# Loading wq by two transfers, over 16 and over 112 rows, in a one-token attention and gated-MLP kernel

## The chip, the cores and the metric

The kernel runs on one core of one Trainium2 chip. Time is the device time in microseconds of one execution, of which three runs of the kernel before are given. A core has five engines with instruction streams of their own (PE for matmuls, DVE, ACT and POOL for element-wise work, SP, which here only issues transfers) and 16 DMA engines which carry the transfers that SP and ACT issue.

## The reference

One token for each of two batch rows. x (2 x 448) is normalized; q = xn @ wq has 16 heads of 256. Attention goes over the last W = 2048 positions of a cache with 8 key and value heads, each used by two query heads; the result, 2 x 4096, is multiplied by wo. Beside it a small MLP of the same normalized x, with silu, gates that product:

```
xn = layernorm(x)
q = (xn @ wq).reshape(B, 1, 16, 256)
scores = q . k_cache[:, :, 8192 - 2048:] * 256 ** -0.5     # heads repeated twice
o = softmax(scores) . v_cache[:, :, 8192 - 2048:]
s = o.reshape(B, 1, 4096) @ wo
g = silu(relu(xn @ w1) @ w2)
out = x + s * g
```

All inputs are bf16. wq is 448 x 4096, w1 448 x 1792, w2 1792 x 448, wo 4096 x 448; the used part of each cache is 2 x 8 x 2048 x 256.

## The kernel before, in words

The work consists mostly in bringing 44 MB into the core's memory: 16.8 MB of keys, 16.8 MB of values, 3.67 MB each of wq and wo, 3.2 MB of w1 and w2. Keys and values come in NQ = 4 rounds of 4 (batch, head) pairs, each round a K tile and a V tile of 128 partitions x 16,384 bf16 (4 MB). There are two buffers for K (kbuf) and two for V (vbuf). The weights borrow them: wq lies in the second V buffer, w1 and w2 in the first, and wo in the first K buffer, after its last K tile has been used.

The order of the instructions on each engine is written out by hand: a small recorder, `_Prog`, appends operations to one list per engine with the operations that they depend on, and `run` turns the dependences into semaphore waits. Each transfer has a semaphore of its own. An operation that waits holds up everything behind it on its engine, SP's issues included. All operations recorded through one helper carry that helper's line in the profile: transfers L36, most matmuls L249.

SP issues all large transfers, in this order: wq (L194), w1 and w2 (L195, L196), K0 and K1, then V0, which waits for the last matmul that reads w1 and w2, then K2, V1, K3, V2, V3 and wo in four parts (L510 to L514), each after the buffer that it overwrites has been read. ACT issues the two loads of x at the beginning and the store of the result.

wq is seen as 896 half rows of 2048, seven of them (SLOTS) on each partition, so that a partition gets one contiguous run of 7 x 2048 bf16 = 28,672 bytes of the matrix:

```
wq_src = A_wq.rearrange("r (hf c) -> (r hf) c", hf=2).rearrange("(p s) c -> p (s c)", s=SLOTS)
```

The steps that wq touches: DVE normalizes x and PE spreads it over the partitions (xr, L255). `do_q` (L261) then waits for wq, xr and a zeroed PSUM bank and runs 28 matmuls that make q, two rescalings on DVE into kt, 16 small matmuls, a copy to qall, and POOL's copies into the block-diagonal stationary tiles qbd. After it on PE come the MLP's matmuls (`do_H`, `do_hT`, `do_F`). Then for each round k: DVE transposes the K tile in eight steps (L343, `do_T`), PE multiplies each by qbd into a score bank (`do_S`), a chain over DVE, PE and ACT takes maximum and exponential, and PE multiplies with the V tile (`do_PV`). The last matmuls (L528) multiply by wo as its four parts land; two DVE operations and a store follow.

Of the kernel before, what the change touches and what calls it, by code (L numbers as in the profile page):

```python
# [11 lines left out]
PE, DVE, ACTE, SP, POOL = "pe", "dve", "act", "sp", "pool"  # L12
# [62 lines left out]
def bass_recurrent_scan__sliding_block_cached__dense_activation_relu__decode_kernel(  # L75
# [24 lines left out]
    SLOTS = 7  # L100
    HC = HD // 2
# [7 lines left out]
    with es:  # L109
        pr = _Prog(nc, es)  # L110
# [7 lines left out]
        def view(t, off, dims, n=128, p0=0, pstep=1):  # L118
            width = t.shape[1]
            return bass.AP(t, p0 * width + off, [[width * pstep, n]] + dims)  # L120
# [42 lines left out]
        wq_sb, w12, wo_sb = vbuf[1], vbuf[0], kbuf[0]  # L163
# [18 lines left out]
        wq_src = A_wq.rearrange("r (hf c) -> (r hf) c", hf=2).rearrange("(p s) c -> p (s c)", s=SLOTS)  # L182
# [8 lines left out]
            d_v[k] = pr.dma(SP, vbuf[k % 2][:, :], kv_src(k, A_v_cache),  # L191
                            [(st["F"], st["q_mm"])[k] if k < 2 else st["PV", k - 2]])

        d_wq = pr.dma(SP, wq_sb[:, 0:SLOTS * HC], wq_src)  # L194
        d_w1 = pr.dma(SP, w12[:, 0:W2], w1_src)  # L195
        d_w2 = pr.dma(SP, w12[:, W2:W2 + 14 * D].rearrange("p (hf f) -> p hf f", hf=2), w2_src)  # L196

# [12 lines left out]
        a_z = [pr.op(ACTE, lambda e, t=t: e.memzero(t[:, :])) for t in (obk[0], obk[1], fbk)]  # L210
# [37 lines left out]
        def mm(out_ap, lhsT, rhs, start, stop=False, **kw):  # L248
            return lambda e: e.matmul(out_ap, lhsT=lhsT, rhs=rhs, start=start, stop=stop,  # L249
                                      skip_group_check=True, **kw)  # L250

        for s in range(SLOTS):
            m_xr = pr.op(PE, mm(mbk[:, 2 * s:2 * s + 2], xg[0:B, 128 * s + 128:128 * s + 256], ident[0:B, 0:B], s == 0),
                         [v_xn, p_id])
        v_xr = pr.op(DVE, lambda e: e.tensor_tensor(  # L255
            out=view(xr, 0, [[4, SLOTS], [2, 2], [1, 2]]), in0=view(mbk, 0, [[2, SLOTS], [0, 2], [1, 2]]),
            in1=view(par8, 0, [[1, SLOTS], [1, 2], [0, 2]]), op=ALU.mult), [m_xr, v_par8])
# [1 line left out]
        st = {"mbk": v_xr}  # L259

        def do_q():  # L261
            deps = [d_wq, v_xr, a_z[0]]
            for s in range(SLOTS):
                for i in range(4):
                    lo = s * HC + i * 512
                    o = pr.op(PE, mm(obk[0][32 * i:32 * i + 4, :], xr[:, 4 * s:4 * s + 4], wq_sb[:, lo:lo + 512],
                                     s == 0, s == SLOTS - 1, tile_position=(0, 32 * i)), deps)
                    deps = []
            st["q_mm"] = o
            for par in range(2):  # L270
                v = pr.op(DVE, lambda e, par=par: e.tensor_scalar(  # L271
                    out=view(kt, 128 * par, [[256, 8], [32, 4], [1, 32]]),
                    in0=view(obk[0], par, [[64, 8], [0, 4], [2, 32]]),
                    scalar1=SCALE, scalar2=None, op0=ALU.mult), [o])
            st["osb", -2] = v
            deps = [v, p_id]
            for h in range(2):
                for cp in range(8):
                    n = 8 * h + cp
                    o = pr.op(PE, mm(nbk[:, 16 * n:16 * n + 16], kt[:, 128 * n:128 * n + 128],  # L280
                                     view(ident, 0, [[2, 2], [32, 4], [1, 2]]), h == 0 and cp == 0,
                                     h == 1 and cp == 7), deps)
                    deps = []
            st["qT"] = o
            st["qall"] = st["nbk"] = pr.op(DVE, lambda e: e.tensor_copy(
                view(qall, 0, [[1, 2], [2, 8], [16, 16]]), view(nbk, 0, [[128, 2], [16, 8], [1, 16]])), [o])
# [169 lines left out]
        load_k(0)  # L456
        load_k(1)
        do_q()
        do_H(0)
        do_H(1)  # L460
# [55 lines left out]
        deps = [st["at", NQ - 1], v_fold]  # L516
        for b in range(2):
            m_at = pr.op(PE, mm(mbk[:, 256 + 32 * b:288 + 32 * b], at_exp[:, 128 * b:128 * b + 128],
                                fold[:, :], b == 0, b == 1), deps + [st["mbk"]])
            deps = []  # L520
        v_at2 = pr.op(DVE, lambda e: e.tensor_copy(at2[:, :], mbk[:, 256:320]), [m_at])  # L521
        deps = [v_at2, st["g"]]
        landed = dict(d_wo)
        for j in range(32):
            deps = deps + [landed.get(j)]
            for i in range(4):
                lo = j * D + i * NCOL
# [3 lines left out]
                deps = []  # L531
# [37 lines left out]
```

## Time and profile before

| | |
|---|---|
| median of three runs | 110.84 us (110.48 to 110.93) |
| the profiled execution | 110.73 us, span 109.3 us |
| moved over SP's queue (q1) | 44.11 MB, 94.6% of 16 engines' span |
| mean rate over the span | 404 GB/s |
| busy PE, DVE, ACT, POOL | 58%, 53%, 11%, 8% of the span |
| granted TensorE clock | 0.875 |

The span goes from the first to the last instruction; the profiled execution's own time is 1.4 us longer than its span. The views used are: the page with its 40 slices, its table of DMA queues and the chain that ended last; the stages (busy time of each engine, DMA share and rate in stretches that one chooses, where a packet is counted in the stretch in which it starts); the instructions in order of time; and the waits. A transfer is cut into packets, which here are one partition's contiguous run each.

### The profile page before, as it was taken

What the parts mean: (1) busy time and instruction counts of PE and PEld (TensorE: products, weight loads), DVE (VectorE), ACT (ScalarE), POOL (GpSimd) and SP (SyncE); (2) the same over time, 40 slices, a digit from 0 to 9 for tenths busy, and PEclk for the clock granted to TensorE, in tenths of its full rate; (3) what the DMA queues carried; (4) which work ended last, traced back from release to release, by engine and by line L of the source; (5) the groups of instructions that cost most, each with busy time, mean ns of one, the idle gap of its engine ahead of it and who ended that gap; (6) DMA issues with size and microseconds to landing.
All of it is one profiled execution on the core that took longest, in us unless ns stands there. A gap on an engine that the chain in (4) does not pass through costs nothing.

```text
span 109.3 us, 1328 instructions
## 1 busy us (share of the span) xinstructions
PE 63.9 (58%) x554; PEld 26.0 (24%) x554; DVE 57.6 (53%) x95; ACT 12.4 (11%) x24; POOL 9.0 (8%) x45
## 2 busy tenths in 40 slices
PE   0010655764089897849481999683089949009491
PEld 0000113133033222323130334241034214003190
DVE  2165047320399999987435999242399943100202
ACT  2970000000000000200050000032000004100200
POOL 6500000720000004000500000000000000000000
PEclk9999999999556999999996559999959999955559
DMA  6898999999999999999999999999999999999940
GB/s 169 346 483 355 431 404 510 408 432 504 390 396 444 492 396 396 456 480 396 399 480 438 396 408 492 432 396 408 504 420 396 420 498 408 396 405 414 407 171 1
DMA packets 2321, 44.19 MB, mean 404 GB/s; under 512 B 266, under 2 KB 396, under 8 KB 908
## 3 DMA queue, kind: packets, MB, share of 16 engines
q1 hardware_dynamic: 2288, 44.11, 94.6%
q8 instruction: 4, 0.07, 0.2%
q10 hardware_dynamic: 28, 0.01, 0.0%
q14 instruction: 1, 0.01, 0.0%
HBM read 44.11 MB, written 0.00 MB: 403 GB/s over the span
## 4 chain that ended last, share of the span: by engine, by line
DMA 70%; DVE 12%; PE 12%; SPq 3%; issue 1%
DMA kbuf<-in_A_k_cache_dram 42%; DMA kbuf<-in_A_wo_dram 28%; DVE kt L343 10%; PE sbk L249 9%; SPq L36 3%; PE obk L249 2%; DVE tmp L331 1%; DVE rm L361 1%; PE mbk L249 0%; PE nbk L249 0%; PE fbk L249 0%; DVE mx L371 0%; DVE tmp L532 0%; PE mbk L366 0%; DVE out_sb L534 0%
## 5 line engine op out<-in xcount | busy, mean ns | idle before, releaser
L249 PE MATMUL sbk<-kt,qbd 128*128 128x512 bf16 x128 | 36.2, 432 | 15.0 <-DVE kt L343 14.5
L343 DVE STREAM_TRANSPOSE kt<-kbuf 128x1024 f32<-128x1024 f32 x32 | 36.9, 1210 | 8.9 <-DMA kbuf<-in_A_k_cache_dram 8.7
L249 PEld LDWEIGHTS sbk<-kt,qbd 128*128 128x128 bf16 x128 | 12.3, 107 | 37.2 <-DVE kt L343 22.5
L249 PE MATMUL obk<-vbuf,pt 128*16 128x512 bf16 x128 | 9.3, 442 | 4.6 <-DMA vbuf<-in_A_v_cache_dram 4.6
L292 POOL COPY qbd<-qall 32x32 bf16<-32x32 bf16 x32 | 5.7, 204 | 44.1 <-PE sbk L249 28.3
L383 ACT ACTIVATE bias<-mbk 128x1 f32<-128x1 f32 x4 | 0.7, 171 | 58.6 <-PE mbk L249 58.6
L433 DVE TENSOR_TENSOR at_exp<-nbk,qmask 128x16 bf16<-128x16 f32 x16 | 1.7, 166 | 10.5 <-PE nbk L249 10.5
L249 PE MATMUL obk<-vbuf,xr 128*4 128x512 bf16 x28 | 3.2, 626 | 3.8 <-DMA vbuf<-in_A_wq_dram 3.8
L392 DVE STREAM_TRANSPOSE pt<-e_sb 128x512 bf16<-128x512 bf16 x4 | 2.8, 711 | 4.7 <-ACT e_sb L387 4.7
L271 DVE TENSOR_SCALAR kt<-obk 128x1024 bf16<-128x1024 f32 x2 | 2.4, 1218 | 5.6 <-PE obk L249 5.6
L249 PEld LDWEIGHTS obk<-vbuf,pt 128*16 128x16 bf16 x128 | 3.1, 98 | 8.5 <-DMA vbuf<-in_A_v_cache_dram 4.7
L249 PE MATMUL mbk<-ident,xg 2*128 2x2 bf16 x7 | 0.3, 164 | 7.9 <-DVE xg L219 7.9
L361 DVE TENSOR_REDUCE rm<-sbk 128x1 f32<-128x512 f32 x4 | 2.7, 682 | 4.0 <-PE sbk L249 4.0
L249 PE MATMUL fbk<-vbuf,xr 128*4 128x448 bf16 x14 | 4.3, 461 | 0.7 <-DVE h_n L304 0.7
L416 ACT ACTIVATE o_sb<-obk,rs 128x512 bf16<-128x512 f32 x4 | 2.7, 687 | 11.1 <-PE obk L249 11.1
L249 PE MATMUL fbk<-kbuf,at 128*17 128x112 bf16 x128 | 3.1, 282 | 0.4 <-DVE at L521 0.3
L249 PEld LDWEIGHTS fbk<-kbuf,at 128*17 128x17 bf16 x128 | 2.7, 128 | 0.7 <-DVE at L521 0.4
L304 DVE TENSOR_SCALAR h_n<-fbk 4x448 bf16<-4x448 f32 x2 | 1.2, 612 | 3.0 <-PE fbk L249 3.0
L387 ACT ACTIVATE e_sb<-sbk,bias 128x512 bf16<-128x512 f32 x4 | 2.7, 687 | 0.1
L249 PE MATMUL mbk<-one_f,mrow 1*128 1x1 f32 x8 | 1.5, 256 | 1.9 <-DVE mrow L374 1.9
L366 PE MATMUL mbk<-ident_f,rm 128*1 128x128 f32 x4 | 1.1, 270 | 2.4 <-DVE rm L361 2.4
L249 PE MATMUL nbk<-fold,o_sb 128*128 128x8 bf16 x16 | 1.0, 170 | 2.2 <-ACT o_sb L416 2.2
(63 smaller groups left out, 34.4 us busy)
## 6 DMA issues: line engine op xcount, KB each, us to landing
kbuf<-in_A_k_cache_dram SPq DMA_DIRECT2D x4, 4096.0 KB, 27.0
vbuf<-in_A_v_cache_dram SPq DMA_DIRECT2D x4, 4096.0 KB, 26.4
vbuf<-in_A_wq_dram SPq DMA_DIRECT2D x1, 3584.0 KB, 11.2
vbuf<-in_B_w_dram SPq DMA_DIRECT2D x2, 1568.0 KB, 16.2
kbuf<-in_A_wo_dram SPq DMA_DIRECT2D x1, 1904.0 KB, 28.2
kbuf<-in_A_wo_dram SPq DMA_DIRECT2D x1, 1008.0 KB, 30.0
kbuf<-in_A_wo_dram SPq DMA_DIRECT2D x1, 448.0 KB, 30.6
kbuf<-in_A_wo_dram SPq DMA_DIRECT2D x1, 224.0 KB, 30.7
```

What stands on the lines that cost most here:

```text
L36: o = _Op(eng, lambda e: e.dma_start(dst, src), [d for d in deps if d is not None], True)
L249: return lambda e: e.matmul(out_ap, lhsT=lhsT, rhs=rhs, start=start, stop=stop, skip_group_check=True, **kw)
L271: v = pr.op(DVE, lambda e, par=par: e.tensor_scalar(out=view(kt, 128 * par, [[256, 8], [32, 4], [1, 32]]), in0=view(obk[0], par, [[64, 8], ...
L292: st["qbd", k] = pr.op(POOL, lambda e, a=a, b=b: e.tensor_copy(view(qbd[k % 2], 24 + 32 * a + 4 * b, [[2, 2], [128, 8], [1, 2]], n=32, p0= ...
L304: st["h_n"] = pr.op(DVE, lambda e: e.tensor_scalar(out=h_n[0:4, u * (FC // 2):(u + 1) * (FC // 2)], in0=fbk[0:4, 0:FC // 2], scalar1=0.0, ...
L343: st["T", k, e] = pr.op(DVE, lambda e: e.transpose(view(dst, lo, [[128, NT // 2], [1, 32]]), view(src, lo, [[128, NT // 2], [1, 32]])), deps)
L361: st["rm", k] = pr.op(DVE, lambda e: e.tensor_reduce(out=rm[k % 2][:, :], in_=sbk[k % 2][:, :], axis=AX.X, op=ALU.max), [st["S", k, 7], st ...
L366: st["rmT", k] = pr.op(PE, lambda e: e.matmul(mbk[0:1, 0:128], lhsT=rm[k % 2][:, :], rhs=ident_f[:, :], start=True, stop=True, is_transpos ...
L387: st["exp", k] = pr.op(ACTE, lambda e: e.activation(e_sb[k % 2][:, :], sbk[k % 2][:, :], ACT.Exp, bias=bias[k % 2][:, 0:1], accum_out=ssum ...
L392: st["pt", k] = pr.op(DVE, lambda e: e.transpose(pt[k % 2][:, :], e_sb[k % 2][:, :]), [st["exp", k], st.get(("PV", k - 2))])
L416: st["osb", k] = pr.op(ACTE, lambda e: e.activation(o_sb[k % 2][:, :], obk[k % 2][:, :], ACT.Copy, scale=rs[:, k:k + 1]), [st["PV", k], st ...
L433: st["at", k] = st["nbk"] = pr.op(DVE, lambda e, b=b, h=h: e.tensor_tensor(out=view(at_exp, 128 * b + 64 * h + 16 * k, [[4, 2], [8, 2], [1 ...
```

## The change

The transfer of wq is issued as two: the first over partitions (rows of wq_src) 0 to 15, the second over 16 to 127. `do_q`, the only reader, waits for both. The number of DMA engines is 16, so the first has one row for each and the second seven.

```
-        d_wq = pr.dma(SP, wq_sb[:, 0:SLOTS * HC], wq_src)
+        d_wq = [pr.dma(SP, wq_sb[lo:hi, 0:SLOTS * HC], wq_src[lo:hi, :]) for lo, hi in ((0, 16), (16, 128))]
         d_w1 = pr.dma(SP, w12[:, 0:W2], w1_src)
...
         def do_q():
-            deps = [d_wq, v_xr, a_z[0]]
+            deps = [*d_wq, v_xr, a_z[0]]
```

SP's list grows by one issue, ahead of w1. The other engines' instructions and their order are the same, but for the wait on one more semaphore ahead of the first matmul of `do_q`.

## The prediction

> **What bounds the kernel now.** I read the page first: span, the lines of DMA by slices, the queues, the chain that ended last.
>
> ```profile
> span 109.3 us, 1328 instructions
> ...
> DMA  6898999999999999999999999999999999999940
> ...
> q1 hardware_dynamic: 2288, 44.11, 94.6%
> ...
> DMA 70%; DVE 12%; PE 12%; SPq 3%; issue 1%
> ```
>
> The 16 DMA engines work in nine tenths or more of nearly every slice, and SP's queue (q1) alone fills 94.6% of sixteen engines' span with 44.11 MB. The gaps stand at both ends: slices of 6 and 8 tenths at the start, 4 and 0 at the end. So I take the kernel as a stream of transfers, and what a change of a transfer is worth as how much later the last byte lands. Next, the stream in stages. The columns of this view are stage, length, busy time of the five engines, granted clock, DMA share and GB/s; a packet is counted in the stage in which it starts.
>
> ```profile
> 0.00:1.60 1.60, 0.00 (x0) 0.00 (x0) 0.00 (x0) 0.00 (x0) 0.83 (x7) 1.00 0.00 0
> 1.60:2.60 1.00, 0.00 (x0) 0.00 (x0) 0.54 (x1) 0.61 (x1) 0.74 (x6) 1.00 1.76 461
> 2.60:3.25 0.65, 0.00 (x0) 0.00 (x0) 0.39 (x3) 0.65 (x1) 0.65 (x1) 1.00 0.00 0
> 3.25:4.25 1.00, 0.00 (x0) 0.00 (x0) 0.00 (x0) 0.99 (x3) 1.00 (x2) 1.00 1.11 459
> 20.00:100.00 80.00, 52.77 (x353) 20.50 (x355) 48.68 (x70) 6.12 (x16) 5.27 (x30) 0.87 1.00 429
> 104.00:104.80 0.80, 0.80 (x44) 0.80 (x40) 0.00 (x0) 0.00 (x0) 0.00 (x0) 0.50 0.84 326
> 104.80:106.30 1.50, 1.50 (x76) 1.50 (x72) 0.00 (x0) 0.00 (x0) 0.00 (x0) 0.51 0.26 91
> ```
>
> The same view of the DMA queues, for the first 3 us alone (packets, MB, share of 16 engines):
>
> ```profile
> q1 hardware_dynamic: 16, 0.46, 58.5%
> ```
>
> Sixteen packets of 0.46 MB in all: each is one whole row of wq as the transfer sees it, 7 x 2048 bf16 = 28,672 bytes, and 16 of them are one per engine. Their time is 58.5% of 16 x 3 us = 28.1 us, a mean of 1.76 us for one. In the middle (20 to 100 us) the stream moves 429 GB/s with every engine busy, 26.8 GB/s an engine, so that the same row takes 28,672 / 26.8 = 1.07 us. I call this a slot. The first row of each engine thus costs 0.69 us more than a slot; nothing new starts from 2.60 to 3.25, and from 3.25 the second rows follow at 459 GB/s. At the end not all engines stop together: after 104.80 the share is 0.26, about four of sixteen, for 1.5 us more. The last piece is late on a few engines only.
>
> **The change part by part.** wq's one transfer of 128 rows (eight to an engine) becomes one of 16 rows (one to an engine) and one of 112 (seven). No byte, no instruction of a compute engine and no wait's target goes; one issue and one completion come. The first matmul still needs both.
>
> *The extra issue.* Instructions in order of time (start us, length, engine and line, in brackets the idle time before and its releaser):
>
> ```profile
> 0.73 0.37 SPq L36 DMA_DIRECT2D vbuf<-in_A_wq_dram  x1
> 0.74 0.54 ACTq L36 DMA_DIRECT2D x_sb<-in_A_x_dram  x1
> 1.17 0.89 SPq L36 DMA_DIRECT2D vbuf<-in_B_w_dram  x2
> 2.06 0.62 DVE L212 BATCH_NORM_STATS2 st<-x_sb 2x6 f32<-2x448 bf16 x1 [2.06 <-DMA x_sb<-in_A_x_dram]
> 2.10 1.51 SPq L36 DMA_DIRECT2D kbuf<-in_A_k_cache_dram  x2
> 9.49 0.18 DVE L255 TENSOR_TENSOR xr<-mbk,par 128x28 bf16<-128x28 f32 x1
> 12.02 3.16 PE L249 MATMUL obk<-vbuf,xr 128*4 128x512 bf16 x28 [3.77 <-DMA vbuf<-in_A_wq_dram]
> 19.57 3.14 POOL L292 COPY qbd<-qall 32x32 bf16<-32x32 bf16 x16 [15.23 <-DVE qall L285]
> 25.74 0.53 SPq L36 DMA_DIRECT2D vbuf<-in_A_v_cache_dram  x1
> ```
>
> The chain that ended last, in order of time (start us, length, what), and SP's own waits (total, times, longest):
>
> ```profile
> 2.10 27.07 DMA kbuf<-in_A_k_cache_dram
> ...
> 29.20 5.75 DVE kt L343 x5
> ...
> 39.68 19.32 DMA kbuf<-in_A_k_cache_dram
> ...
> 75.98 30.68 DMA kbuf<-in_A_wo_dram
> ```
>
> ```profile
> SPq L36 <- PE fbk L249: 22.1, 1, 22.1
> ```
>
> One issue takes 0.37 to 0.45 us of SP (0.89 for two). The second wq transfer is issued at about 1.17 instead of w1, and w1, w2, K0 and K1 go 0.44 us later. I cost this at nothing. No byte moved before 1.60, 0.9 us after wq's issue, so the seven rows would be there at about 2.1, while the first rows end no earlier than 1.6 + 1.07 = 2.7; behind them the engines hold eight slots, 8.6 us, before w1 is wanted. If that cover were gone it would cost 0.44 us. The next issue on SP, V0, waits 22.1 us for the last matmul of the second block and goes at 25.74 anyway.
>
> *Later issues.* Those that wait (V0, K2, V1, wo) move with their releasers. V0 goes at 25.74, but K0 lands only at 2.10 + 27.07 = 29.17 and the 4.19 MB of K1 (128 x 16,384 bf16) behind it are 9.8 us at 429 GB/s: 13 us of work ahead. K2 takes 19.32 us to land for 9.8 us of data, so 9.5 us stand ahead of it, and wo (4096 x 448 bf16, 3.67 MB, 8.6 us) takes 30.68. A shift under 9 us leaves no engine dry; the stream just slides. The compute around it slides too: if wq lands 6 us later, the first matmul starts near 18, and its chain to the first use of K0, which took from 12.02 to 22.71 (the copies into qbd; with the second block to 25.74), ends near 29, that of the block near 32, ahead of K0 at 29.2 + 5 or more and long before V0 would be missed.
>
> *x on ACT's queue.* It is issued with wq. Should its two short rows fall behind a long first row, bn_stats goes from 2.06 to some 6 us, and xr from 9.67 to about 13.7. It had 12.02 - 9.67 = 2.35 us to spare and gains what wq loses. Nothing.
>
> *Where the 16 rows land.* This is the term that decides. Before, the engines write sixteen sets of eight partitions at once, each at 26.8 GB/s. Now all sixteen write partitions 0 to 15 at once. If the way into the memory belongs to sets of partitions, as many ways as sets, these rows share some ways while others stand idle. No row shows such sharing, so it is bounded: every row its own way, one slot, 1.07 us; all on one way, 16 slots, 17.1 us. What is nearest is unknown within this factor of 16; I take the middle of the ratio, four ways with four rows each: 4 slots, 4.28 us, that is +3.21 for the stream, since the ways that idle are as full later as before. Of it the slow start pays 0.69 (a row held to a quarter of the rate no longer notices a slow first fetch): net +2.52. [...]
>
> *The 112 rows.* [...] Bounds: no meeting, 0; every row met by one other, seven slots more, 7.5 us. Neither is near any row; I take half, 3.7 us for the slowest engine, which is the one that counts, as a transfer is complete with its last row.
>
> *The end.* Today about four engines are up to 1.5 us later than the rest. The engine that is now held up may be one of them (then all is added) or not (then 1.5 is hidden): I take 0.75 off.
>
> Sum: 3.21 - 0.69 + 3.7 - 0.75 = +5.5 us. The profiled execution took 110.73 us (span 109.3 and 1.4 around it), 0.1 under the median of 110.84: 110.73 + 5.5 = **116.2 us**. With the second transfer's bounds and the end's 0 to 1.5: +1.0 to +10.0, 111.7 to 120.7. I would look for it between 113.9 and 119.0.
>
> **The rivals.**
>
> *Even second transfer.* The sharing lies in the 16 rows only, and the 112 run as freely as today. For it: all 128-row transfers run at full rate. Against: seven rows are not eight. 3.21 - 0.69 - 0.75 = +1.8: 112.5 us.
>
> *Nothing happens.* Ways into the memory don't depend on partitions, and the first rows cost 1.76 us as before. For it: no row of this profile shows two engines in each other's way once the start is over. The issue's 0.44 is hidden: 110.8 us.
>
> *Faster.* The 0.69 us over a slot is the price of starting eight rows per engine from cold; with one short transfer first, the rows come at a full slot. For it: the mean of 1.76 and the empty 2.60 to 3.25. Against: by the second row the rate is full, whatever stands queued, so the price may be of first touch and not of length. 110.73 - 0.69 = 110.0 us. It decides from where the mean first packet is under 1.2 us (0.55 us off all engines is 0.5%), with no sharing.
>
> *Rows dealt out in turn.* If row r goes to engine r mod 16, each round of the second transfer meets like the first: eight rounds of 3 slots too many, 25.7 us, 25 net of the start: 135.7 us. Against: today's full rate needs engines to keep to sets of partitions, and a dealt order would break that.
>
> [...]
>
> **How the numbers follow.** My forecast, shared ways in both transfers, has 0.58; sharing in the first alone 0.18; nothing 0.10; faster 0.07; dealt out 0.07. What a measurement of this kernel can tell from no change is about 0.5%, 0.55 us. Slower: 0.58 + 0.18 + 0.07 = 0.83; same 0.10; faster 0.07. The range must take in the case of no change to leave out no more than two in ten: 110.6 to 119.0, with faster, dealt out and some 0.05 of the forecast's upper end outside.
>
> **What would show it.** Right: in the first 3 us still 16 packets, but of some 4 us each instead of 1.76; near 110 GB/s up to about 6 us; then a stage well under 429 GB/s until wq is in; the first matmul at 17 to 20 instead of 12.02; K0's transposes start near 34.5 instead of 29.20, and each later landing is later by the same 5 us, with 429 GB/s in the middle; the end of the stream more ragged. Wrong: first packets of 1 to 2 us (no sharing: the second or third rival, told apart by their mean); first packets of 4 us but the first matmul near 15 (even second transfer); first matmul past 35 (dealt out). The first matmul late and the end not later would mean that the stream had room which I don't see.

## The result, and the profile after

The changed kernel takes 117.62 us (median of six runs, 117.47 to 117.88) against 110.73 us (110.37 to 110.93): a ratio of 1.0635, with a 95% interval of 1.062 to 1.065, or 6.9 us more. It is slower, as forecast; 1.4 us more than the 116.2 us forecast, and within the ranges given.

The page of the changed kernel (117.62 us, span 116.3): the same work on the compute engines, and the same full DMA engines. What changed is what they moved.

```profile
span 116.3 us, 1330 instructions
...
DMA  9869979999999899999999999999999999999950
GB/s 158 158 158 316 296 195 337 416 492 417 473 394 490 383 417 462 406 485 394 417 476 394 468 394 417 485 394 473 394 428 473 394 473 400 406 406 420 418 215 1
...
q1 hardware_dynamic: 2304, 44.11, 95.0%
```

The same row of rates before (slices of 2.7 us):

```profile
GB/s 169 346 483 355 431 404 510 408 432 504 390 396 444 492 396 396 456 480 396 399 480 438 396 408 492 432 396 408 504 420 396 420 498 408 396 405 414 407 171 1
```

This is the trap of this trace: by the share of busy time nothing is wrong with the transfers, neither in the slices nor in q1's 95.0% (94.6% before). The rate tells it: 158 GB/s in the first three slices of 2.9 us, of which only the first was as low before (169, then 346 and 483), under 340 until the eighth, and then the old level. Engines that are held up count as busy here: a stage at 173 GB/s has a DMA share of 1.03, the middle at 431 GB/s one of 1.00.

The stages of the changed kernel (stage, length, busy time of PE, of its weight loads, of DVE, ACT and POOL, granted clock, DMA share, GB/s; a packet counts where it starts):

```profile
1.60:6.90 5.30, 0.00 (x0) 0.00 (x0) 1.39 (x5) 4.84 (x7) 2.48 (x7) 1.00 1.03 173
6.90:17.10 10.20, 0.34 (x7) 0.26 (x7) 2.70 (x11) 0.77 (x1) 0.00 (x0) 1.00 1.02 270
17.10:22.00 4.90, 2.39 (x24) 0.84 (x28) 0.00 (x0) 0.00 (x0) 0.00 (x0) 1.00 0.92 344
46.00:106.00 60.00, 39.73 (x247) 15.63 (x249) 37.63 (x57) 5.86 (x15) 2.93 (x16) 0.90 1.00 431
112.00:113.30 1.30, 1.19 (x52) 0.94 (x48) 0.00 (x0) 0.00 (x0) 0.00 (x0) 0.50 0.19 73
```

and of the kernel before:

```profile
1.60:16.00 14.40, 3.50 (x35) 1.06 (x35) 4.87 (x16) 5.61 (x7) 2.47 (x7) 1.00 0.99 404
40.00:100.00 60.00, 39.76 (x251) 15.53 (x253) 36.56 (x56) 5.86 (x15) 2.83 (x16) 0.88 1.00 431
```

In the middle both move 431 GB/s, so a stage's loss is its length less its bytes at that rate. In the changed kernel the first stage, in which 32 rows of wq start, moves 173 x 5.30 = 917 KB, worth 2.1 us: 3.2 us lost. The other 96 rows move at 270 GB/s: 10.2 us for 6.4 us of data, 3.8 lost. While w1 begins, 1.0 more. Together 8.0 us, against 14.4 - 404 x 14.4 / 431 = 0.9 us at the start of the kernel before: 7.1 us, which is the 7.0 us by which the span grew. Nothing is lost later.

The landings (KB, us from issue to landing), first before, then the two of the changed kernel, and the compute around them:

```profile
vbuf<-in_A_wq_dram SPq DMA_DIRECT2D x1, 3584.0 KB, 11.2
vbuf<-in_A_wq_dram SPq DMA_DIRECT2D x1, 3136.0 KB, 18.3
vbuf<-in_A_wq_dram SPq DMA_DIRECT2D x1, 448.0 KB, 5.9
```

```profile
1.63 1.35 SPq L36 DMA_DIRECT2D vbuf<-in_B_w_dram  x2
2.34 0.61 DVE L212 BATCH_NORM_STATS2 st<-x_sb 2x6 f32<-2x448 bf16 x1 [2.34 <-DMA x_sb<-in_A_x_dram]
9.49 0.18 DVE L255 TENSOR_TENSOR xr<-mbk,par 128x28 bf16<-128x28 f32 x1
19.61 3.16 PE L249 MATMUL obk<-vbuf,xr 128*4 128x512 bf16 x28 [11.37 <-DMA vbuf<-in_A_wq_dram]
36.45 4.62 DVE L343 STREAM_TRANSPOSE kt<-kbuf 128x1024 f32<-128x1024 f32 x4 [4.24 <-DMA kbuf<-in_A_k_cache_dram]
```

wq as a whole landed 11.2 us after its issue; now its smaller part takes 5.9 us and the larger 18.3. The first matmul goes from 12.02 to 19.61 (+7.6), K0's transposes from 29.20 to 36.45 (+7.25), the span's end by 7.0. The delay is made once and carried to the end.

### The profile page after: what moved, and what is told of

Read it like the earlier page. It is cut to its first block, busy times and chain, and to the rows that moved or that the text cites. A ratio compares the mean times of both kernels' runs of the same rounds, so it can differ in the third digit from the quotient of the medians.

```text
span 116.3 us, 1330 instructions
## 1 busy us (share of the span) xinstructions
PE 63.7 (55%) x554; PEld 25.6 (22%) x554; DVE 57.5 (49%) x95; ACT 12.4 (11%) x24; POOL 9.1 (8%) x45
## 4 chain that ended last, share of the span: by engine, by line
DMA 72%; DVE 18%; PE 4%; SPq 3%; issue 1%
DMA kbuf<-in_A_k_cache_dram 45%; DMA kbuf<-in_A_wo_dram 27%; DVE kt L343 16%; SPq L36 3%; PE obk L249 2%; PE sbk L249 1%; PE fbk L249 1%; DVE tmp L331 1%; DVE rm L361 1%; PE mbk L249 0%; PE nbk L249 0%; DVE mx L371 0%; DVE tmp L532 0%; PE mbk L366 0%; DVE out_sb L534 0%
## 5 line engine op out<-in xcount | busy, mean ns | idle before, releaser
L249 PEld LDWEIGHTS sbk<-kt,qbd 128*128 128x128 bf16 x128 | 12.6, 108 | 36.9 <-DVE kt L343 21.3
L249 PEld LDWEIGHTS obk<-vbuf,xr 128*4 128x4 bf16 x28 | 0.8, 115 | 12.8 <-issue 12.8
L249 PEld LDWEIGHTS fbk<-kbuf,at 128*17 128x17 bf16 x128 | 2.0, 104 | 1.6 <-DMA kbuf<-in_A_wo_dram 1.2
## 6 DMA issues: line engine op xcount, KB each, us to landing
vbuf<-in_A_wq_dram SPq DMA_DIRECT2D x1, 3136.0 KB, 18.3
```

## The experiments

All times are medians, with the ratio to the kernel before run on the same chip (110.48 to 110.54 us) and its 95% interval.

**The same two sizes, cut by columns.** Each transfer covers all 128 partitions.

```
-        d_wq = pr.dma(SP, wq_sb[:, 0:SLOTS * HC], wq_src)
+        d_wq = [pr.dma(SP, wq_sb[:, lo:hi], wq_src[:, lo:hi]) for lo, hi in ((0, 1792), (1792, SLOTS * HC))]
...
-            deps = [d_wq, v_xr, a_z[0]]
+            deps = [*d_wq, v_xr, a_z[0]]
```

> wq by two transfers of the same sizes as in the changed kernel (0.46 and 3.2 MB), but cut by columns, so that both write all 128 partitions. Theory (engines meet where a transfer covers few partitions): no meeting, the first matmul at 12 us as before, 110.7 us, within 0.5. Rival (the price is of a second transfer, or of a short one at the start): as the changed kernel, 117 us or more, first matmul near 19.6. A third reading (a short first transfer starts the engines sooner): below 110.2.

110.62 us, ratio 1.001 (1.000 to 1.002). The first matmul starts at 12.05:

```profile
12.05 3.16 PE L249 MATMUL obk<-vbuf,xr 128*4 128x512 bf16 x28 [3.81 <-DMA vbuf<-in_A_wq_dram]
```

A second transfer of wq, and a short first one, cost about 0.1 us (0.2 at the upper end of the interval) and bring nothing. Here each row goes in two packets, which the changed kernel's rows do not; the two runs with eight transfers below have packets of one size. Otherwise only the place is left of the change: which partitions each part covers. The reading by which a short transfer starts the engines sooner falls too.

**Two halves of 64 rows.**

```
+        d_wq = [pr.dma(SP, wq_sb[lo:hi, 0:SLOTS * HC], wq_src[lo:hi, :]) for lo, hi in ((0, 64), (64, 128))]
```

> wq by rows 0 to 63 and 64 to 127: four rows for each engine in each half. [...] Rival (the price is of the 16 short rows or of the odd seven): neither is here, 110.7 to 111.5 us.

119.86 us, 1.085 (1.0834 to 1.0866): +9.4, with no short transfer and no odd seven. Some 0.3 us of it is a later start: the two issues took 1.20 us of SP instead of 0.85 in the changed kernel, and wq's first packet starts at 2.08 us instead of 1.76. In the stages, wq moves at 200 GB/s:

```profile
4.00:19.20 15.20, 0.34 (x7) 0.26 (x7) 3.16 (x12) 3.60 (x5) 0.33 (x1) 1.00 0.97 200
```

That is somewhat under half of 431 (0.46), for 64 neighbouring partitions at a time.

**The 112 rows first, the 16 last.**

```
+        d_wq = [pr.dma(SP, wq_sb[lo:hi, 0:SLOTS * HC], wq_src[lo:hi, :]) for lo, hi in ((0, 112), (112, 128))]
```

> The same two sizes in the other order: 112 rows from partition 0 first, then the 16 rows of partitions 112 to 127. Theory: the meeting goes by place, not by order, so about the same 117 us as the changed kernel (116 to 118.5). Rival (the short transfer at the cold start is what costs): 110.7 to 112.

119.02 us, 1.0777 (1.0753 to 1.0801). The order at the cold start is not what costs. It is 1.4 us worse than the changed kernel, which the theory did not give beyond its upper end of 118.5. The stages show where: up to 17.10 us the two have lost about the same (6.9 us here, 7.0 in the changed kernel, reckoned as above; here 260 GB/s to 6.90 and 230 to 17.10), and in the next stage, in which w1 begins beside the last rows of wq, this run moves 264 GB/s where the changed kernel moves 344.

```profile
17.10:22.00 4.90, 1.87 (x20) 0.69 (x24) 0.00 (x0) 0.00 (x0) 0.00 (x0) 1.00 0.80 264
```

That is 1.9 us lost there against 1.0. In the packet records of the traces the first sixteen packets of w1 took 1.0 to 1.9 us each, 0.7 to 0.9 in the changed kernel and 0.47 before. One part has a reason in the forecast's own working: the 16 rows no longer take over the slow start's 0.7 us. How the two go together was not tested.

**The 16 rows alone, as an addition.** A transfer into kt stands ahead of the old transfer of wq.

```
+        d_ex = pr.dma(SP, kt[0:16, 0:SLOTS * HC], wq_src[0:16, :])
         d_wq = pr.dma(SP, wq_sb[:, 0:SLOTS * HC], wq_src)
...
-            deps = [d_wq, v_xr, a_z[0]]
+            deps = [d_wq, d_ex, v_xr, a_z[0]]
```

> The kernel before, with one transfer more ahead of wq: the same 16 rows into partitions 0 to 15 of kt, a tile that is free then; the rows are loaded twice and the copy is not used. Its bytes alone are one slot: +1.07 us, 111.8. Theory: four slots, 4.28 us, less the 0.69 of the slow start which it takes over: +3.6, 114.3 us. If the first transfer is the whole of the changed kernel's loss: 1.07 + 6.9 = +8, 118.7.

113.96 us, 1.0316 (1.0301 to 1.0332): +3.5 where 3.6 was expected. One slot of this is bytes (1.06 us, by the run with 128 extra rows below), so the 16 rows lose 2.4 us net of the start. That is about a third of the changed kernel's 6.9, and not the whole.

**Writing side or reading side.** The same 16 source rows go to every eighth partition; then every eighth source row goes to partitions 0 to 15.

```
+        d_ex = pr.dma(SP, kt[0:128:8, 0:SLOTS * HC], wq_src[0:16, :])
```

> As the run with 16 extra rows, but the same 16 source rows go to every eighth partition of kt (0, 8, ... 120). [...] Rival (the price lies on the reading side, 16 engines in 0.46 MB of the source): nothing changes against partitions 0 to 15, the same time as that run.

112.74 us, 1.0195 (1.0178 to 1.0212).

```
+        d_ex = pr.dma(SP, kt[0:16, 0:SLOTS * HC], wq_src[0:128:8, :])
```

> The counterpart: 16 extra rows into partitions 0 to 15 of kt, but read from every eighth row of the source (0, 8, ... 120). Theory (the writing side decides): the same time as with the 16 neighbouring source rows, about 114.3 us. Rival (the reading side): 111.8 us, one slot more than before.

114.18 us, 1.0334 (1.0319 to 1.035). Spreading the source changes nothing (+3.6 against +3.5); spreading the destination takes 1.3 us off. The place that is written decides. Part of the +2.2 us of the spread destination is a longer first issue, 0.60 us here and 0.37 for 16 neighbours, behind which the first packet starts at 2.12 us instead of 1.74:

```profile
0.73 0.60 SPq L36 DMA_DIRECT2D kt<-in_A_wq_dram  x1
```

This one run at the cold start leaves open at what rate the two places are written; the next two show it.

**Eight times 16 neighbours, and eight times 16 at every eighth partition.** Two kernels with the same number of transfers and the same sizes; both load wq as it was. The second spreads the source rows too, which by the run before changes nothing.

```
+        d_wq = [pr.dma(SP, wq_sb[lo:hi, 0:SLOTS * HC], wq_src[lo:hi, :]) for lo, hi in [(16 * i, 16 * i + 16) for i in range(8)]]
```

> wq by eight transfers of 16 rows, each over 16 neighbouring partitions, one row for each engine at a time. Theory: each takes four slots, 8 x 4.28 = 34.2 us instead of 8.6, less the slow start's 0.7: +25, 135.7 us, and the first matmul near 37. If the later ones overlap (an engine on its next row while others still write the last): less, down to 8.6 us for wq if nothing meets: 110.7. Seven more issues of 0.4 us delay w1 and what follows by 3 us, which wq's own time covers.

132.67 us, 1.1998 (1.1962 to 1.2033).

```
+        d_wq = [pr.dma(SP, wq_sb[i:128:8, 0:SLOTS * HC], wq_src[i:128:8, :]) for i in range(8)]
```

> wq by eight transfers of 16 rows as in the run with eight times 16 neighbours, with the same number of issues and the same sizes, but each over every eighth partition (i, i + 8, ... i + 120). There each took 3.91 us, four rows on a way at 0.98 us. [...] If the price goes by the number of small transfers and not by place: 132.7 us again.

119.62 us, 1.0827 (1.0795 to 1.0858). A stage of each, of the neighbours first:

```profile
4.50:32.00 27.50, 0.34 (x7) 0.26 (x7) 3.17 (x12) 3.12 (x4) 0.00 (x0) 1.00 1.01 117
```

```profile
3.50:20.50 17.00, 0.34 (x7) 0.26 (x7) 3.17 (x12) 4.11 (x6) 0.83 (x1) 1.00 0.98 209
```

Sixteen neighbours move at 117 GB/s, 458,752 / 117 = 3.92 us for a transfer: 0.27 of 431, near the four ways of sixteen that the forecast took as an estimate. At every eighth partition it is 209 GB/s, 2.2 us: 0.48 of 431, near the 200 of the halves, and not the 1.07 us of a slot. Which partitions share a way, if any do, is not shown; the runs give the rates by the partitions that are written. The number of small transfers is the same in both and explains none of the 13 us between them.

**The 112 rows alone, and all 128, as an addition.**

```
+        d_ex = pr.dma(SP, kt[16:128, 0:SLOTS * HC], wq_src[16:128, :])
```

> The kernel before, with a transfer of rows 16 to 127 into partitions 16 to 127 of kt ahead of wq (loaded twice, the copy not used). Its bytes alone are seven slots, 7.5 us: 118.2. Theory: the uneven sevens meet and add half as much again or a little more, 3.7 to 5.4 us, less the slow start's 0.7: 121 to 123 us. If the 112 rows run freely: 118.2, and the changed kernel's whole loss would be of its 16 rows.

123.13 us, 1.1157 (1.1134 to 1.118).

```
+        d_ex = pr.dma(SP, kt[:, 0:SLOTS * HC], wq_src)
```

> The kernel before, with all 128 rows loaded once more into kt ahead of wq, the copy not used: 3.67 MB, 0.46 MB more than in the run with 112 extra rows, which took 123.1 us. Theory (only transfers that don't cover the 128 partitions evenly meet): eight slots, 8.56 us, nothing else: 119.1 us, 4 us less than with fewer bytes. If the extra 5 us of the 112 rows come from a longer queue or from loading wq twice: 1.07 more than there, 124.2 us.

118.97 us, 1.076 (1.0742 to 1.0778): +8.44 us, eight slots of 1.055. Sixteen more rows make the load 4.2 us shorter. The stages show why, the 112 rows above (these and the first 23 of wq start in it), the 128 with wq below:

```profile
1.60:15.80 14.20, 0.34 (x7) 0.26 (x7) 4.09 (x15) 5.61 (x7) 2.48 (x7) 1.00 1.02 273
```

```profile
1.60:19.00 17.40, 0.34 (x7) 0.26 (x7) 4.10 (x15) 5.61 (x7) 2.47 (x7) 1.00 1.02 422
```

273 GB/s, as in the changed kernel's second stage (270), against 422. Of the +12.6 us of the 112 rows 7 x 1.055 = 7.4 are bytes; 5.2 us are lost although all sixteen engines have work (a DMA share of 1.02). That they are lost to rows meeting on a way was the forecast's estimate and is not shown; no record tells which rows an engine takes, as a packet's record does not name its partition. Dealt out in turn they would be seven times 16 neighbours, 7 x 3.92 = 27.4 us by the run above, which the 12.6 exclude.

## Why the prediction was right, point by point

*The stream as the bound*: right. A delay made in the first 20 us stood unchanged at the end, at an unchanged 431 GB/s in between; no engine ran dry (a DMA share of 1.00).

*The extra issue, x, and the compute that slides*: right in effect. The cut by columns prices a second issue at about 0.1 us. In the changed kernel the pair w1 and w2 took 1.35 us of SP where it took 0.89, more than the 0.44 us assumed for the whole step, and stayed covered. x arrived at 2.34 instead of 2.06 and xr at 9.67 as before.

*The 16 rows, +3.21 - 0.69 = +2.52*: right, 2.4 us by the run that adds them alone. Four ways were only the middle of a ratio. The run of eight times 16 neighbours comes near four (117 of 431 GB/s, 0.27), but no row of the kernel before had said so, and that the choice hit it is luck as far as those rows go. The sign that I named, first packets of some 4 us and 110 GB/s, came weaker. The queue's view of the first 3 us has

```profile
q1 hardware_dynamic: 16, 0.46, 100.4%
```

which is a mean of 3.0 us for a first packet, against 1.76 before. From the start of the first (1.76) to the end of the last (5.55) the 16 rows took 3.8 us, but engines that were done went on to their second row; two rows of each engine took 5.3 us together at 173 GB/s. The full four slots, 3.92 us, show for each packet where 16-row transfers follow each other.

*The 112 rows, +3.7*: right that they lose, and too small. No run shows the term of 3.7 us, half of a bound, or why the rows lose; what the runs showed in its place is 4.8 and 5.2 us. The changed kernel loses 3.8 us from 6.90 to 17.10 and 1.0 while w1 begins, 4.8 us, of which the kernel before lost little at that place (0.9 in all, of which the first term has used 0.69). The run that adds them alone gives 5.2. Half of the bound of 7.5 was a choice without a row; 4.8 to 5.2 us are about two thirds of it.

*The end, -0.75*: wrong. I let the hold-up hide behind the engines that finish late, as if it hit some engines and not others. After the change, the last stage has a share of 0.19 over 1.3 us, about as ragged as before (0.26 over 1.5): all engines came later by about the same 7 us. The packet records agree: the last sixteen rows of wq end between 17.2 and 18.5 us, and between 10.7 and 11.7 before. The run that adds the 16 rows alone shows the spreading by itself. There the next row of each engine belongs to wq's transfer over all 128 partitions, in which the later rows take 1.06 us each:

```profile
4.30:5.60 1.30, 0.00 (x0) 0.00 (x0) 0.00 (x0) 1.28 (x3) 0.03 (x1) 1.00 1.66 353
```

Sixteen rows start in this stretch (353 x 1.30 = 459 KB), and they took 1.66 x 1.30 = 2.2 us each in the mean, 1.7 to 2.5 by the packet records: every one was slowed, though their transfer covers all 128 partitions. By what path the slowing reaches them stays open.

Put together: 2.4 to 2.5 + 4.8 - 0 is 7.2 to 7.3 by the stages' terms, less the 0.2 that the kernel before lost at its start beyond the 0.69, against 6.9 measured and 5.5 forecast. The two additions run alone sum to 2.4 + 5.2 = 7.6, 0.7 more than together; why they cost less one behind the other stays open.

*The rivals*: "even second transfer" falls by the 5.2 us of the 112 rows alone; "nothing happens" by the result; "faster" by the cut by columns, where a short first transfer brought no gain; "rows dealt out in turn" by the result, and its price is roughly confirmed where I built that case: +22.1 us measured for eight rounds of 16 neighbours, 25 forecast, the difference being 3.92 us a round and not 4.28.

Two parts are no loss by themselves: the cut by columns cost about 0.1 us. The loss goes with the partitions covered.

No run beat the kernel before; the nearest, the cut by columns, is the same within 0.2%.

## What to carry to other kernels

Sixteen busy DMA engines need not give sixteen engines' worth of bandwidth (270 of 431 GB/s here): look at GB/s beside the share, stage by stage. If a load must be split, cut it along the free axis, so that each part covers all 128 partitions (about 0.1 us here); a cut along the partitions cost 6.9 to 22 us on a load of 8.6. It is worth measuring the rate of any transfer under 128 partitions, above all where the transfers are the bound.

## What the runs showed of the hardware that was not expected

Sixteen neighbouring rows moved at somewhat more than a quarter of the full rate, 117 GB/s against 431 / 4 = 107.8. Sixteen rows at every eighth partition, and 64 neighbouring rows, moved at somewhat less than half of it, 209 and 200 GB/s against 215.5. And a transfer of 112 rows moved slower, at 270 to 273 GB/s, than fourteen of sixteen engines' worth (377), though all sixteen were busy throughout (DMA shares of 1.02).
